# An FNet block with a GeGLU feed-forward on one core: two places for GpSimd's sums, two loads a step sooner, one tile of the second DFT a step later

## The chip, the cores and the metric

The kernel runs on one core of a Trainium2 chip. The metric is the time of one execution on the device, in microseconds (us). The engines of a core have short names in the profile: PE is TensorE (PEld its weight loads), DVE is VectorE, ACT is ScalarE, POOL is GpSimd and SP is SyncE, whose instruction queue issues every DMA of this kernel. Each engine works through its own instructions strictly in the order of the program and waits on semaphores for the others; so does SP, and a DMA that has to wait for a free buffer holds up every DMA behind it.

## The reference

```python
x = A_x                                    # 2048 x 448
n = layernorm(x)
a = n @ dft_hid_re.T ; b = n @ dft_hid_im.T      # DFT along the hidden dimension
h = x + dft_seq_re @ a - dft_seq_im @ b          # DFT along the sequence, real part
g = layernorm(h)
out = h + (gelu(g @ w_gate) * (g @ w_up)) @ w_down   # w_gate, w_up: 448 x 1792
```

All arrays are float32.

## The kernel before, in words

Every product of two float32 matrices is made of three float16 products: each operand is split into a high half (a float16 copy, made by ScalarE in `hi_part`, L107) and a low half (what the copy left out, a float16 made by VectorE in `lo_part`, L110). TensorE takes high by high, high by low and low by high into the same PSUM bank. Splitting the operands in time is what keeps ScalarE and VectorE busy.

The kernel does the DFT along the sequence first, on the normed x (16 tiles `xs` of 128 rows, two halves each), and the DFT along the hidden dimension second. The work before the feed-forward is a loop of 64 steps (`N_STEPS`, L416; the loop is at L848). In each step TensorE multiplies one *unit* of the sequence matrix, 128 x 1024 elements:

- Steps 0 to 15 go over the 16 tiles of x for two of the eight row pairs `p` at once.
- Steps 16 to 31 go over `p` = 2 and 3, eight steps each: four units for `part` 0, four for `part` 1 (`step_of`, L419). A step has 24 matmuls.
- Steps 32 to 63 (`FAST` = 32, L452) do `p` = 4 to 7 with Strassen's seven products on half-size blocks (`fast_mm`, L516; the diff's "seven-product passes"). A step has 42 matmuls. For this the unit needs sums of its blocks (`fast_sums`, VectorE), its raw blocks split (`fast_raw`) and the sums split (`fast_split`); and x needs sums of its own, the T operands of `xs`: for each of the eight pairs `j` of x tiles, `t_sums(j)` (L567) makes them on GpSimd in seven operations, in place in the two arrays `tx[j]`; `t_hi(j)` (ScalarE) and `t_lo(j)` (VectorE) split them.

**Units and slots.** `seq_load(n)` (L424) puts unit n, in two halves for n of 16 and more, into one of the five slots of the tag `wr`; the sums of a seven-product unit take a slot of the same five. The loop (L859) loads unit n+5 in step n, up to unit 33; from unit 34 on, the loads stand behind `fast_split`, two units ahead. The step whose code prepares a seven-product unit is in `fast_at` (L812): step 28 for unit 32, 30 for unit 33, 31 for unit 34, and from step 33 on unit n+2.

**Tiles of the second DFT.** Row pair `p` gives a tile of 256 rows, in two halves g = 0 and 1. When `p` is through, `z_turn(p)` (L662) transposes its result by four DMA transposes into the one tile `z`. `hid_seed(p, g)` (L705, the copy at L708) is a ScalarE copy of the residual x into a PSUM bank; `hid_mm(p, g)` (L720) adds 21 matmuls to it; `hid_out(p, g)` (L710) has ScalarE copy the bank out as h, with its sum (L716), scale the mean (L717) and sum the squares (L718). Both halves use the single bank `tr`, so `hid_seed(p, 1)` stands behind `hid_out(p, 0)`. `ffn_rstd` (L198; a root on ScalarE, a reciprocal on VectorE, the rest on GpSimd), `h_store` and, for the first four tiles, the operands of the feed-forward follow: `ffn_bias` (GpSimd), `ffn_norm_act` (ScalarE), `ffn_sums` (VectorE), `ffn_split` (ScalarE and VectorE) and four DMA transposes `ffn_transpose`. Tiles `p` = 0 to 3 are also called pairs (0,0), (0,1), (1,0) and (1,1) there; "pair 1" is (0,1).

**Weights.** Eight of the fourteen column blocks f of the gate and up weights are prepared during these steps (`DFT_F`, L745): loaded, summed, split in two parts and stored.

**The order** is written out by hand in two tables: `early[n]` is done in step n ahead of its matmuls, `after[n, half]` behind the first or second half of them. What is entered first is done first. For tile p, the lists at L780 to L796 give the step `m` of `hid_mm(p, 0)`, the place `last` of `hid_mm(p, 1)`, and the steps n0, n1, n2 of norm, sums and split. `m1`, one step behind `last`, places `ffn_rstd` and `h_store`. `t_sums(j)` is in `early`, `t_hi(j)` behind the second half of that step, `t_lo(j)` behind the first half of the next.

**The place of `tx`.** Before the change it is one tile under the tag `xh2`, so `t_sums` of one pair waits until `t_lo` of the pair ahead has read it. The x tiles (tag `xt`, three slots) are last read in step 13.

After the 64 steps come the gate and up products (L1321 onward) and the down products with the output; the change does not touch them.

Of the kernel before, what the change touches and what calls it, by code (L numbers as in the profile page):

```python
# [9 lines left out]
F32 = mybir.dt.float32  # L10
# [3 lines left out]
P = 128  # L14
S, D, DF = 2048, 448, 1792
# [17 lines left out]
def kernel(  # L33
# [45 lines left out]
    ring = ctx.enter_context(tc.tile_pool(name="ring", bufs=2))  # L79
# [215 lines left out]
    def ffn_split(q, j):  # L295
        ffn_hi(q, j)
        ffn_lo(q, j)
# [15 lines left out]
    dft = seq.enter_context(tc.tile_pool(name="dft", bufs=1, side="right"))  # L313
# [51 lines left out]
    xt, xs, norm_x = {}, {}, {}  # L365
# [53 lines left out]
    def step_of(n):  # L419

        k, qq = divmod(n - NT, 4)
        return 2 + k // 2, k % 2, qq

    def seq_load(n):  # L424
        wr[n] = dft.tile([P, 8 * P], F32, tag="wr", bufs=5, name=f"wr{n}")
        if n < NT:
            nc.sync.dma_start(wr[n].rearrange("p (b t) -> p b t", b=4), w_seq[8 * (n % 2) + n // 2])
            return
        p, part, qq = step_of(n)
        for i in range(2):  # L430
            dst = wr[n][:, i * 4 * P : (i + 1) * 4 * P].rearrange("p (g t) -> p g t", g=2)
            nc.sync.dma_start(dst, w_seq[8 * p + 2 * qq + i][:, 2 * part : 2 * part + 2, :])
# [19 lines left out]
    FAST = N_STEPS - 32  # L452
# [112 lines left out]
    tx = {}  # L565

    def t_sums(j):  # L567
        t = ring.tile([P, 2, D], F32, tag="xh2", bufs=1, name=f"tx{j}")
        tx[j] = [t[:, k] for k in range(2)]
        for k in range(2):  # L570
            i = 2 * j + 1 - k
            G.tensor_add(tx[j][k], xs[i][:, 0], xs[i][:, 1])  # L572
        (o1, o2), (e1, e2) = [(t[:, 0:HD], t[:, HD:D]) for t in tx[j]]
        G.tensor_sub(o1, o2, o1)
        G.tensor_sub(o2, e2, o2)
        G.tensor_sub(e2, o1, e2)
        G.tensor_add(e1, e1, e2)
        G.tensor_scalar(e1, e1, -1.0, None, op0=ALU.mult)
# [120 lines left out]
    def h_tile(q, j):  # L699
        hp[q, j] = pair_tile(f"hx{q}_{j}", 2 * (q - 2) + j if q > 1 else j)  # L700
        nc.sync.dma_start(hp[q, j], xr[q // 2, 2 * (q % 2) + j])
# [3 lines left out]
    def hid_seed(p, g):  # L705

        y = ys[p, g] = ps_tr.tile([P, 512], F32, tag="tr", name=f"y_{p}_{g}")
        A.activation(y[:, :D], hp[p // 2, p % 2][:, g, :], AF.Copy, scale=sign_of(p, g) * D_SC)  # L708
# [31 lines left out]
    def h_store(q, j):  # L740
        nc.sync.dma_start(h_dram[2 * q + j], hp[q, j])
# [8 lines left out]
    def at(where, n, *what):  # L750
        where.setdefault(n, []).extend(what)
# [26 lines left out]
    for p, (n, half) in enumerate(turns):  # L778
        b, j = divmod(p, 2)
        m = (19, 24, 29, 36, 44, 52, 60)[p]  # L780
        last = ((20, 0), (25, 0), (30, 0), (38, 0), (48, 0), (56, 0), (61, 1))[p]
        m1 = last[0] + 1
        at(early, m - 4, lambda b=b, j=j: h_tile(b, j))
        at(early, m - 2, lambda p=p: hid_seed(p, 0))
        for g in range(2):

            place = last if g else (m, 0)
            at(after, place, lambda p=p, g=g: hid_mm(p, g), lambda p=p, g=g: hid_out(p, g))
            if g == 0:
                at(after, (m, 0), lambda p=p: hid_seed(p, 1))  # L790
        at(after, (n, half), lambda p=p: z_turn(p))
        at(early, m1 + p // 3 if p < 5 else N_STEPS - 7 + p, lambda b=b, j=j: ffn_rstd(b, j))
        at(after, (m1, 0), lambda b=b, j=j: h_store(b, j))
        if b < 2:

            n0, n1, n2 = ((21, 22, 23), (26, 27, 29), (36, 37, 38), (44, 45, 46))[p]  # L796
            at(early, n0, lambda b=b, j=j: ffn_bias(b, j), lambda b=b, j=j: ffn_norm_act(b, j, hp[b, j]))
            at(early, n1, lambda b=b, j=j: ffn_sums(b, j))
            at(early, n2, lambda b=b, j=j: ffn_split(b, j))
            for k in range(4):  # L800
                at(after, (n2 + 1 + k // 2, k % 2), lambda b=b, j=j, k=k: ffn_transpose(b, j, (k,)))
# [1 line left out]
    at(after, (N_STEPS - 6, 0), lambda: gu.update({JIT_F[0]: Weights(JIT_F[0], JIT_F[0] % 3)}))  # L803
    at(early, N_STEPS - 1, gelu_table)
    at(after, (N_STEPS - 2, 0), lambda: down_load(0), lambda: down_load(1))
    for j, n in ((6, 14), (7, 16), (0, 18), (1, 20), (4, 22), (5, 24), (2, 28), (3, 31)):
        at(early, n, lambda j=j: t_sums(j))
        at(after, (n, 1), lambda j=j: t_hi(j))
        at(after, (n + 1, 0), lambda j=j: t_lo(j))
# [38 lines left out]
    for n in range(N_STEPS):  # L848
        if n == 0:
            for key in first:  # L850
                seq_acc(*key, last=key == first[-1])
        elif n >= FAST and n % 4 == 0:
            fast_begin(n)
        elif n >= NT and n % 4 == 0:
            for g in range(2):
                seq_acc(*step_of(n)[:2], g)
        if n + 3 < NT:
            x_load(n + 3)
        if n + 3 < FAST:  # L859
            seq_load(n + 5)  # L860

        if 0 < n < FAST - 3:
            seq_hi(n + 3)
        if 0 < n < NT - 2:
            x_rstd(n + 2)
            x_hi(n + 2)
            x_norm(n + 2)
        if 0 < n < NT - 3:
            x_stats(n + 3)
        if n == 0:  # L870
            seq_lo(2)
        if n + 3 < FAST:
            seq_lo(n + 3)
        if n in fast_at:
            unit = fast_at.index(n) + FAST
            fast_sums(unit)
            while last_lo:
                last_lo.pop()()

            if n < FAST or n % 4 < 3:  # L880
                fast_raw(unit)
                fast_split(unit)
                if unit + 2 < N_STEPS:
                    seq_load(unit + 2)
        if n == 0:
            x_stats(3)
            x_lo(2)
        if 0 < n < NT - 2:
            x_lo(n + 2)
        for what in early.get(n, ()):  # L890
            what()
        if n >= FAST:

            last = n % 4 == 3
            one = [(i, k) for k in range(7) for i in range(2)] if last else [(i, k) for i in range(2) for k in range(7)]
            if n % 4 == 0 and n > FAST:

                one = [(i, k) for i in range(2) for k in range(5)] + [(i, k) for i in range(2) for k in (5, 6)]  # L900
            for m, (i, k) in enumerate(one):
                fast_mm(n, i, k)
                if last and i == 1 and k in (0, 2, 4, 6):
                    fast_out(n, k)
                    if n < N_STEPS - 1:
                        unit = n + 2
                        if k == 2:
                            fast_raw(unit)
                        elif k == 4:
                            fast_split(unit)  # L910
                            if unit + 2 < N_STEPS:
                                seq_load(unit + 2)
                if m in (6, 13):
                    for what in after.get((n, m // 7), ()):
                        what()
            continue

        if n < NT:
            one = [(key, n - n % 2 + key[0], 2 * (2 * key[1] + key[2]) + n % 2, n) for key in first]
            if n == 0:  # L920

                order = [(0, m) for m in (0, 2, 1)] + [(1, m) for m in range(3)]
                one = [(*a, (m,)) for jj, m in order for a in one[4 * jj : 4 * jj + 4]]
            elif n < 6:
                one = [(*a, (m,)) for m in (0, 2, 1) for a in one]
            else:
                one = [(*a, range(3)) for a in one]
        else:
            p, part, qq = step_of(n)
            one = [  # L930
                ((p, part, g), n, 4 * i + 2 * g + c, 4 * qq + 2 * i + c, range(3))
                for i in range(2)
                for g in range(2)
                for c in range(2)
            ]
            if qq == 3:

                one.sort(key=lambda a: a[0])
        for half in range(2):
            for key, unit, block, c, terms in one[half * len(one) // 2 : (half + 1) * len(one) // 2]:  # L940
                seq_mm(key, ws[unit], block, c, terms)
                if c == NT - 1 and 2 in terms and (n < NT or block in (5, 7)):
                    z_out(*key)
            for what in after.get((n, half), ()):
                what()
# [376 lines left out]
    for t in range(NF):  # L1322
        w = gu.get(t + 2) if t + 2 in JIT_F else None
        n = PREP_AT.get(t)
# [88 lines left out]
    for t in range(NF, N_GU):  # L1413
# [37 lines left out]
        if ends:  # L1451
            p = now[-1] // NC
# [21 lines left out]
        for p, t0 in ended.items():  # L1474
            each = 3 if p < 3 else 2
            n = each * (t - t0)
# [106 lines left out]
```

## Time and profile before

| | us |
|---|---|
| median of 3 runs (lowest, highest) | 709.0 (708.27, 710.05) |
| the profiled execution | 708.71 |
| its span, first to last instruction | 706.9 |
| TensorE busy | 695.0 |
| VectorE busy | 571.7 |
| ScalarE busy | 393.7 |
| GpSimd busy | 163.4 |

The mean granted TensorE clock was 0.995 of full speed. All times in the profile are counted from the start of the span. A row of a timeline gives start, duration, engine, line, operation, what it writes and reads, and how many instructions were merged; brackets at its end give the idle time of the engine just before it and what ended that. A row of the waits gives the waiting engine and line, what it waited for, the total, the number of times and the longest.

### The profile page before, as it was taken

Reading aid. Unit: us, or ns where it says so; the run is one execution under the profiler, and the core shown is the slowest. Engines: PE = TensorE matmul, PEld = TensorE weight load, DVE = VectorE, ACT = ScalarE, POOL = GpSimd, SP = SyncE. Lnnn points to the kernel's source line nnn. Section 1 sums busy time; section 2 is a strip of 40 time slices with the busy share of each in tenths; the row PEclk is TensorE's granted clock in tenths of the full one; section 3 lists DMA queues with packets and bytes.
Section 4 is the critical chain, followed back from the end, with each engine's and each line's share of the span. In section 5 each row is a group of like instructions: output and inputs, shape, how many; then the busy total and the mean of one; then the engine's idle time right before and its main releaser. Section 6 shows DMA issues by size and latency. Waiting matters only on the chain.

```text
span 706.9 us, 13957 instructions
## 1 busy us (share of the span) xinstructions
PE 695.0 (98%) x5308; PEld 514.2 (73%) x5308; DVE 571.7 (81%) x1137; ACT 393.7 (56%) x781; POOL 163.4 (23%) x183
## 2 busy tenths in 40 slices
PE   9999999997999999999999999999999999999998
PEld 5555545553788899888744444469999999999997
DVE  7998887969599898997456798877778876899886
ACT  5776555556566475654536666655546454555531
POOL 0004447540300100000213333511020111232224
PEclk9999999998999999999999999999999999999999
DMA  8788759997655829575674878797778985877612
GB/s 273 239 239 287 204 188 275 283 274 235 142 172 153 209 76 208 168 185 168 169 235 156 288 248 262 205 312 236 243 236 300 259 283 177 314 284 259 240 54 79
DMA packets 113731, 155.81 MB, mean 220 GB/s; under 512 B 61696, under 2 KB 78208, under 8 KB 113664
## 3 DMA queue, kind: packets, MB, share of 16 engines
q1 hardware_dynamic: 113664, 154.92, 71.3%
q8 instruction: 41, 0.67, 0.4%
q14 instruction: 26, 0.21, 0.1%
HBM read 106.66 MB, written 34.34 MB: 199 GB/s over the span
## 4 chain that ended last, share of the span: by engine, by line
PE 82%; DVE 4%; DMA 4%; POOL 3%; SPq 2%; ACT 2%; issue 2%; DVEq 0%; ACTq 0%; POOLq 0%
PE acc_f L521 17%; PE acc_d L1245 15%; PE pY L1041 15%; PE acc L641 10%; PE pX L1041 9%; PE pZ L1041 9%; PE y L727 7%; DMA wr<-in_w_seq_dram 2%; DVE gu_w L114 1%; POOL tx L572 1%; DMA gu_raw<-in_w_gu_dram 1%; DVE zs L114 1%; DMA w_dram<-gu_w 1%; SPq L666 1%; DVE t L112 1%
## 5 line engine op out<-in xcount | busy, mean ns | idle before, releaser
L1041 PEld LDWEIGHTS <-gw 128*128 128x128 f16 x1365 | 133.1, 98 | 43.0 <-DMA gw<-w_dram 0.2
L641 PE MATMUL acc<-xs,ws 128*128 128x448 f16 x768 | 146.6, 353 | 0.3 <-DVE xs L149 0.3
L521 PEld LDWEIGHTS <-ws 128*128 128x128 f16 x1344 | 128.8, 98 | 3.2 <-issue 1.6
L641 PEld LDWEIGHTS <-ws 128*128 128x128 f16 x768 | 75.0, 98 | 70.6 <-ACT ws L108 0.4
L1135 POOL TENSOR_TENSOR hs<-hs,c 128x256 f32<-128x256 f32 (+1 forms) x42 | 59.9, 1426 | 247.2 <-ACT c L1133 182.3
L1245 PE MATMUL acc_d<-wd,dn_w 128*128 128x224 f16 x1008 | 110.7, 259 | 0.0
L1245 PEld LDWEIGHTS <-dn_w 128*128 128x128 f16 x1008 | 96.9, 98 | 1.9
L521 PE MATMUL acc_f<-t,ws 128*128 128x224 f16 x768 | 92.1, 259 | 1.4 <-DVE t L112 1.4
L1041 PE MATMUL pY<-hops,gw 128*128 128x256 f16 (+1 forms) x595 | 90.2, 294 | 0.0
L114 DVE SCALAR_TENSOR_TENSOR ws<-wr,ws 128x768 f16<-128x768 f32 (+2 forms) x66 | 71.0, 1077 | 19.0 <-ACT ws L108 18.6
L727 PE MATMUL y<-wh,z 128*128 128x448 f16 x336 | 68.6, 362 | 5.6 <-ACT y L708 5.6
L521 PE MATMUL acc_f<-xs,ws 128*128 128x224 f16 x576 | 73.5, 259 | 0.0
L108 ACT ACTIVATE ws<-wr 128x768 f16<-128x768 f32 (+2 forms) x66 | 60.3, 914 | 11.7 <-DMA wr<-in_w_seq_dram 11.1
L1041 PE MATMUL pX<-hops,gw 128*128 128x256 f16 (+1 forms) x385 | 61.7, 294 | 0.0
L1041 PE MATMUL pZ<-hops,gw 128*128 128x256 f16 (+1 forms) x385 | 61.7, 294 | 0.0
L727 PEld LDWEIGHTS <-z 128*128 128x128 f16 x336 | 33.5, 100 | 37.1 <-issue 9.0
L1086 ACT ACTIVATE pY<-pX 128x256 f32<-128x256 f32 (+1 forms) x42 | 18.4, 439 | 67.0 <-PE pX L1041 66.6
L108 ACT ACTIVATE ws<-sums 128x512 f16<-128x512 f32 x64 | 38.6, 623 | 25.2 <-DVE sums L471 20.8
L1051 DVE SCALAR_TENSOR_TENSOR c<-pZ,u 128x256 f32<-128x256 f32 (+1 forms) x42 | 21.5, 511 | 35.6 <-PE pZ L1041 19.6
L1041 PEld LDWEIGHTS <-gu_w 128*128 128x128 f16 x273 | 26.6, 98 | 31.9
L1097 ACT ACTIVATE u<-pY 128x256 f32<-128x256 f32 (+1 forms) x42 | 19.1, 454 | 53.3 <-PE pY L1041 53.2
L112 DVE TENSOR_TENSOR dn_w<-dn_s,dn_w 128x640 f16<-128x640 f32 x48 | 42.3, 880 | 1.5 <-ACT dn_w L108 1.4
(146 smaller groups left out, 1003.5 us busy)
## 6 DMA issues: line engine op xcount, KB each, us to landing
gw<-w_dram SPq DMA_DIRECT2D x35, 896.0 KB, 6.4
wr<-in_w_seq_dram SPq DMA_DIRECT2D x100, 256.0 KB, 4.1
hid_dram<-hs SPq DMA_DIRECT2D x27, 512.0 KB, 6.0
hid<-hid_dram SPq DMA_DIRECT2D x54, 256.0 KB, 5.4
w_dram<-gu_w SPq DMA_DIRECT2D x14, 896.0 KB, 4.7
gu_raw<-in_w_gu_dram SPq DMA_DIRECT2D x28, 384.0 KB, 5.3
wr<-in_w_seq_dram SPq DMA_DIRECT2D x14, 512.0 KB, 5.6
x<-in_x_dram SPq DMA_DIRECT2D x16, 224.0 KB, 4.0
```

Source lines behind the costliest of these rows:

```text
L108: A.activation(dst, src, AF.Copy, scale=scale)
L112: V.tensor_sub(dst, src, hi)
L114: V.scalar_tensor_tensor(dst, src, scale, hi, op0=ALU.mult, op1=ALU.subtract)
L521: PE.matmul(fast_sum(n, k), fast_a(n, i, lw, a), fast_b(j, lx, b), start=j == 0 and m == 0 and k in (0, 1, 3, 5), stop=j == NT // 2 - 1 an ...
L641: PE.matmul(acc[key][:, :D], w[:, lw, block * P : (block + 1) * P], xs[c][:, lx, :], start=c == 0 and m == 0, stop=c == NT - 1 and m == 2,)
L727: PE.matmul(y[:, :D], z[p][:, lz, k, g * P : (g + 1) * P], wh[:, lw, k, :], start=p == NP - 1 and k == 0 and m == 0, stop=k == 6 and m == ...
L1041: PE.matmul(ps, w[:, wl, wa + ws, :], ops[:, m + ms, :], start=first and n == 0, stop=last and n == len(terms) - 1, skip_group_check=True,)
L1051: V.scalar_tensor_tensor(dst, ps, SC, other, op0=ALU.mult, op1=ALU.add)
L1086: A.activation(self.Y, self.X, AF.Copy)
L1097: A.activation(self.u2, self.Y, AF.Copy, scale=SC)
L1135: G.tensor_mul(c22, c22, self.cols(self.c12))
L1245: PE.matmul(ps, w[:, la, a, :], wd[n][:, lb, b, :], start=n == 0 and m == 0 and opens, stop=n == NC - 1 and m == 2, skip_group_check=True,)
```

## The change

- `t_sums` uses the `xh2` tile for the first, third, fifth and seventh pair of its order (6, 7, 0, 1, 4, 5, 2, 3), and two slots of the `xt` ring for the others.
- The last `t_sums` (pair 3) is entered in step 30 instead of 31, and with it its `t_hi` and `t_lo`.
- `hid_mm(2, 1)` and its `hid_out` stand behind the first half of step 31 instead of 30; with them `ffn_rstd(1, 0)` and `h_store(1, 0)` move from step 31 to 32.
- For pair 1, `ffn_bias` and `ffn_norm_act` move from step 26 to 27, `ffn_sums` from 27 to 28, `ffn_split` from 29 to 32, and the four transposes from behind steps 30 and 31 to behind 33 and 34.
- Step 26 loads units 31 and 32, step 27 loads unit 33, step 28 none by this loop. Before, they were loaded one each in steps 26, 27 and 28 (units 31, 32 and 33).

```diff
     def t_sums(j):
-        t = ring.tile([P, 2, D], F32, tag="xh2", bufs=1, name=f"tx{j}")
-        tx[j] = [t[:, k] for k in range(2)]
+        if len(tx) % 2 == 0:
+            t = ring.tile([P, 2, D], F32, tag="xh2", bufs=1, name=f"tx{j}")
+            tx[j] = [t[:, k] for k in range(2)]
+        else:
+            tx[j] = [dft.tile([P, 1, D], F32, tag="xt", bufs=3, name=f"tx{j}_{k}")[:, 0, :] for k in range(2)]
...
-        last = ((20, 0), (25, 0), (30, 0), (38, 0), (48, 0), (56, 0), (61, 1))[p]
+        last = ((20, 0), (25, 0), (31, 0), (38, 0), (48, 0), (56, 0), (61, 1))[p]
...
-            n0, n1, n2 = ((21, 22, 23), (26, 27, 29), (36, 37, 38), (44, 45, 46))[p]
+            n0, n1, n2 = ((21, 22, 23), (27, 28, 32), (36, 37, 38), (44, 45, 46))[p]
...
-    for j, n in ((6, 14), (7, 16), (0, 18), (1, 20), (4, 22), (5, 24), (2, 28), (3, 31)):
+    for j, n in ((6, 14), (7, 16), (0, 18), (1, 20), (4, 22), (5, 24), (2, 28), (3, 30)):
...
-        if n + 3 < FAST:
-            seq_load(n + 5)
+        for unit in range(n + 5 + (n > FAST - 6), min(n + 6 + (n > FAST - 7), FAST + 2)):
+            seq_load(unit)
```

## The prediction

> **What bounds the kernel now.** I read the page first, then the waits of TensorE, then its timeline around each wait, and last the timelines of ScalarE, VectorE, GpSimd and the DMA queue of SyncE backwards from there.
>
> ```profile
> span 706.9 us, 13957 instructions
> ...
> PE 695.0 (98%) x5308; PEld 514.2 (73%) x5308; DVE 571.7 (81%) x1137; ACT 393.7 (56%) x781; POOL 163.4 (23%) x183
> ```
> ```profile
> PE y L727 <- ACT y L708: 5.6, 2, 4.2
> PE acc_f L521 <- DVE t L112: 1.4, 1, 1.4
> ```
>
> TensorE is busy for 98% of the span, so only its holes can be won. All its waits behind the opening are three: two for a seed of the second DFT (`hid_seed`, L708: the residual, copied into the PSUM bank by ScalarE ahead of `hid_mm`), one for the low half of a T operand (`t_lo`). The change touches what leads up to all three. Their true size is in TensorE's timeline (start, duration, what):
>
> ```profile
> 98.42 4.70 PE L641 MATMUL acc<-xs,ws 128*128 128x448 f16 x24
> 104.53 4.13 PE L727 MATMUL y<-wh,z 128*128 128x448 f16 x21 [1.41 <-ACT y L708]
> ...
> 139.19 18.32 PE L641 MATMUL acc<-xs,ws 128*128 128x448 f16 x96
> 157.35 4.14 PE L727 MATMUL y<-wh,z 128*128 128x448 f16 x21
> 161.33 4.70 PE L641 MATMUL acc<-xs,ws 128*128 128x448 f16 x24
> 170.25 6.53 PE L727 MATMUL y<-wh,z 128*128 128x448 f16 x21 [4.22 <-ACT y L708]
> 176.62 6.97 PE L641 MATMUL acc<-xs,ws 128*128 128x448 f16 x36
> ...
> 189.47 0.74 PE L521 MATMUL acc_f<-xs,ws 128*128 128x224 f16 x6
> 190.04 0.26 PE L521 MATMUL acc_f<-t,ws 128*128 128x224 f16 x1
> 191.72 0.93 PE L521 MATMUL acc_f<-t,ws 128*128 128x224 f16 x8 [1.42 <-DVE t L112]
> ```
> ```profile
> 170.00:176.00 6.00, 5.75 (x18) 2.46 (x18) 5.90 (x12) 2.23 (x4) 0.00 (x0) 0.57 0.77 195
> ...
> 192.00:345.00 153.00, 153.00 (x1435) 137.64 (x1434) 131.30 (x212) 88.61 (x169) 8.08 (x23) 1.00 0.62 169
> ```
>
> A step of 24 matmuls takes (157.35 - 139.19) / 4 = 4.54 us; a `hid_mm` takes 161.33 - 157.35 = 3.98.
> - First seed, tile 0, second half: due at 98.42 + 4.54 = 102.96, started at 104.53. Loss 1.57.
> - Second seed, tile 2, second half: due at 165.87, started at 170.25. Loss 4.38.
> - After it the 21 matmuls took 176.62 - 170.25 = 6.37 instead of 3.98, at a granted clock of 0.57 from 170 to 176. Loss 2.39. (The gaps of about 1.5 us have no such tail.)
> - T operand: six matmuls take 0.57, so the next was due at 190.14 and came at 191.72. Loss 1.58.
>
> (The two rows by window give the busy time of TensorE, its weight loads, VectorE, ScalarE and GpSimd, then the granted clock, the DMA share and GB/s.)
>
> Sum 9.92 us. From 192 to 345 TensorE is busy for 153.00 of 153.00, so what is won before 192 shifts the rest as a whole.
>
> **Part 1, the second `hid_mm` of tile 2 a step later, and pair 1's split from step 29 to 32.** Why was the seed late? ScalarE, with the slots ahead of it:
>
> ```profile
> 159.06 0.84 ACT L108 ACTIVATE ws<-wr 128x768 f16<-128x768 f32 x1 [3.49 <-DMA wr<-in_w_seq_dram]
> ...
> 166.31 0.81 ACT L108 ACTIVATE xs<-xn_h 128x256 f16<-128x256 f32 x2
> ...
> 168.02 0.52 ACT L716 ACTIVATE hx<-y 128x448 f32<-128x448 f32 x1
> ...
> 169.66 0.55 ACT L708 ACTIVATE y<-hx 128x448 f32<-128x448 f32 x1
> ```
>
> Tile 2's first `hid_mm` ended at 161.33, but ScalarE got to its `hid_out` only at 168.02: it had stood 3.49 us for the load of unit 32, and had pair 1's split (166.31 to 168.02, 1.71 us) in front. The seed was there at 170.2. The new place, behind half of step 31, is due 4.54 us later, at 165.87 + 4.54 = 170.41, or 168.84 with the first stall gone. Without the split the seed comes at 170.2 - 1.7 = 168.5 even if nothing else improves. So this stall should go, and the slow clock with it: -4.38 and -2.39.
>
> The step the move issues is 21 matmuls, three ScalarE operations, then the moments, `h_store` and `ffn_rstd`, each a step later. `hid_seed` of tile 3 is at step 34, three steps behind: free. `z_turn(3)` on SP refills the single z tile and must now wait for a `hid_mm` that ends near 172.8, but its last two transposes wait for step 31's own drain, near 176, anyway: free. Behind it on SP stand `h_store` and unit 37's load, needed four steps on.
>
> The split lands in step 32, in front of unit 35 on ScalarE and VectorE. Bounds: on TensorE at least 0; at most its own length if unit 35 is just in time, 1.7 on ScalarE and 2.5 on VectorE:
>
> ```profile
> 167.13 0.42 DVE L112 TENSOR_TENSOR xs<-xn_h,xs 128x256 f16<-128x256 f32 x1
> ...
> 169.64 1.16 DVE L112 TENSOR_TENSOR t<-tx,t 128x448 f16<-128x448 f32 x2
> ...
> 189.56 1.03 DVE L114 SCALAR_TENSOR_TENSOR gu_w<-gu_raw,gu_w 128x512 f16<-128x512 f32 x2 [4.74 <-ACT gu_w L108]
> ...
> 196.31 0.69 DVE L471 TENSOR_TENSOR sums<-wr 128x512 f32<-128x512 f32 x1
> ...
> 198.70 1.22 DVE L114 SCALAR_TENSOR_TENSOR ws<-sums,ws 128x1024 f16<-128x1024 f32 x1
> ```
>
> The split's low halves run from 167.13 to 169.64: 2.5 us. Unit 36 took VectorE from 196.31 to 199.92: 3.6 us for one unit. It was needed at about 201.1: step 32 opened at 176.62 + 36 x 0.189 = 183.4, so 70 of the 84 matmuls of steps 32 and 33 were through by 190.14; the other 14 and two steps of 42, at 0.0955 each, follow on 191.72. That is 1.2 us of slack, and no wait. In the new order step 32 opens at 183.4 - 1.57 - 4.38 - 2.39 = 175.1. Step 31's last drain is out some 1.4 later by my estimate (a copy and a subtraction); from 176.5 I walk VectorE: 1.03 for half a gate weight, 2.5 for the split, 3.6 for unit 35: 183.6. Step 35 is due at 175.1 + 3 x 4.0 = 187.1. Slack 3.5, more than it had. I take 0.
>
> **Part 2, units 32 and 33 loaded a step sooner.** The same loads, moved on SP past the load of weights for f = 0 and the store of pair 1 (which come about 1 us later; the weights are wanted at step 30), and unit 33 past the store of weights for f = 3:
>
> ```profile
> 148.90 1.08 SPq L432 DMA_DIRECT2D wr<-in_w_seq_dram  x2
> 150.08 1.01 SPq L323 DMA_DIRECT2D gu_raw<-in_w_gu_dram  x2
> 151.19 0.38 SPq L741 DMA_DIRECT2D h_dram<-hx  x1
> 151.61 1.44 SPq L432 DMA_DIRECT2D wr<-in_w_seq_dram  x2
> ```
>
> Unit 32 goes out at 150.0 instead of 151.6, ahead of 768 + 448 KB. It landed at 159.06; I estimate 155.5 to 157.5. Bounds: 0 to 3.49 us off ScalarE's wait. The five slots are handed out in the same order, and the slots in question hold units 27 and 28, read two steps before, so nothing new is waited for. On TensorE it is worth 0 by itself, since part 1 already covers the seed; it makes the margin.
>
> **Part 3, two places for GpSimd's sums; the last ones at step 30.** The odd ones go into the ring of x tiles, dead since step 13.
>
> ```profile
> 178.59 0.19 POOL L204 TENSOR_SCALAR r_h<-mv_h 128x2 f32<-128x2 f32 x1 [20.70 <-ACT y L718]
> ...
> 182.71 2.02 POOL L572 TENSOR_TENSOR tx<-xs 128x448 f32<-128x448 f16 x2
> ...
> 187.63 0.77 POOL L578 TENSOR_SCALAR tx<-tx 128x224 f32<-128x224 f32 x1
> ```
>
> The last sums waited in GpSimd's queue behind `ffn_rstd` of tile 2, which waited 20.70 us for `hid_out`; their low halves came at 191.7. Now they are queued ahead of that and have their own place: ready near 164, due at step 33's second half, near 182. -1.58, with 15 us to spare.
>
> ```profile
> POOL tx L572 <- DVE t L112: 19.9, 2, 11.8
> ```
> ```profile
> 99.61 0.58 ACT L108 ACTIVATE t<-tx 128x448 f16<-128x448 f32 x1 [2.06 <-POOL tx L578]
> ...
> 102.29 0.53 ACT L716 ACTIVATE hx<-y 128x448 f32<-128x448 f32 x1
> ...
> 103.93 0.55 ACT L708 ACTIVATE y<-hx 128x448 f32<-128x448 f32 x1
> ```
> ```profile
> 134.63 0.55 ACT L708 ACTIVATE y<-hx 128x448 f32<-128x448 f32 x1
> ```
>
> GpSimd waited 19.9 us for its one place, and ScalarE, in order, for GpSimd. The longest of its waits was 11.8; without them the high half at 99.61 is done some 10 us sooner; tile 0's `hid_out`, at 102.29, can follow TensorE's end at 98.42 closely, and with the 2.2 us from 102.29 to the seed's end it is there at about 101, before 102.96. -1.57. Less sure: tile 1's seed ended at 135.18, just when TensorE wanted it (139.19 - 3.98 = 135.21); it must come 1.57 us earlier as well, or the stall returns there.
>
> What part 3 adds is company: the second sums now run from about 69 to 77, beside VectorE's work ahead of the drain of step 15.
>
> ```profile
> 69.74 1.23 DVE L114 SCALAR_TENSOR_TENSOR ws<-wr,ws 128x1024 f16<-128x1024 f32 x1 [0.32 <-DMA wr<-in_w_seq_dram]
> ...
> 75.36 2.33 DVE L114 SCALAR_TENSOR_TENSOR zs<-acc,zs 128x448 f16<-128x448 f32 x4 [0.59 <-ACT zs L108]
> ```
> ```profile
> L328 DVE TENSOR_TENSOR gu_s<-gu_raw x14: 544/556/1014, 70.9 to 441.2; 128x384 f32<-128x384 f32 x14
> ```
>
> An operation of 0.556 at the median took up to 1.014. Of the 5.0 us that VectorE works between 69.74 and its wait of 0.59, the factor 1.8 makes 0 to 4.1 more; I take 2.5, as not all will meet a sum. The first bank was emptied at 75.36 + 0.58 and is wanted at step 16's opening, 98.42 - 3.98 - 3.5 x 4.54 = 78.6: slack 2.6. I put 0.3 on TensorE, between 0 and 1.5. [...]
>
> **Sum.** 4.38 + 2.39 + 1.58 + 1.57 - 0.3 = 9.6 us. The profiled execution took 708.71 (span 706.9), 0.3 under the median of 709.0; on the median it gives 709.0 - 9.6 = 699.4.
>
> **Rivals.**
> - A, the first stall is given back, at tile 0's seed or at tile 1's: 699.4 + 1.57 = 701.0. For: 135.18 against 135.21. Against: ScalarE's waits for GpSimd go ahead of both. 0.14.
> - B, a new wait at units 35 to 37: VectorE comes late to step 32, the split in front. 2 to 4.4 us, if the clock holds: 701.4 to 703.8. For: 1.2 us of slack before. Against: the walk above. 0.12.
> - C, the change doesn't do what it says: unit 32 lands no sooner behind full queues, TensorE's earlier arrival uses up the step, and the seed is as late as before; only the T operand's 1.58 is won: 707.4. Against: the split alone makes 1.7. 0.05.
> - D, slower: SP becomes the bound. Pair 1's four transposes now stand between the loads of units 37, 38 and 39, and wait for the split. It decides once SP gets to unit 38 after about 193 (step 38 is due near 203: 187.1 + 3 x 4.0 + 3.98; less 3.6 of preparation and, by the 159.06 - 151.61 of unit 32, up to 7 of landing); I expect 184 to 187, as its slot is emptied with unit 35's raw half near 183. Past that point three units in a row would each cost a stall of 4.4 and 2.4 of slow clock: 699.4 + 20 = 720. 0.04.
> - E, the sums shut VectorE out. The seven operations of one tile take 182.71 to 188.40, 5.7 us; if VectorE stood still for them all between 69 and 77, the first bank would come at 75.36 + 5.7 + 0.58 - 0.59 = 81.05, 2.5 after it is wanted: 699.4 + 2.5 - 0.3 = 701.6. For: the 1.014. Against: GpSimd's own operations stretch as well, so the two share the loss. 0.05.
>
> **How the numbers follow.** Forecast 0.60, its own range 698.0 (708.27, the fastest run, less 9.92, rounded down) to 700.4. Nine tenths of that, A, E and two thirds of B lie between 698.0 and 703.0: 0.54 + 0.14 + 0.05 + 0.08 = 0.81. A measurement here tells about 0.3%, 2.1 us, from no change: forecast, A, B and E are faster (0.91), C is the same (0.05), D slower (0.04).
>
> **What would show it.** TensorE's waits should list neither L708 nor `t` behind L521; the second `hid_mm` of tile 2 should take 4.1 near 169; the granted clock should stay at 1.00 from 157 to 192; step 32 should open near 175 instead of 183.2; GpSimd's last sums should be done by 165; the wait of 3.49 on ScalarE should shrink. I am wrong if a new wait for `ws` or `sums` stands between 175 and 205, or if L708 is there again at 102 or 133.

## The result

| | before | changed |
|---|---|---|
| median, us (lowest, highest; 4 runs each) | 709.05 (708.27, 710.05) | 699.6 (698.65, 699.91) |
| ratio to before, 95% interval | | 0.9864 (0.9847 to 0.9881) |
| the profiled execution, us | 708.71 | 699.87 |
| its span, us | 706.9 | 698.1 |

The forecast was 699.4. The head of the page of the changed kernel, and all its waits of TensorE (waiting engine and line, what it waited for, total, times, longest):

```profile
span 698.1 us, 13955 instructions
...
PE 693.5 (99%) x5308; PEld 514.3 (74%) x5308; DVE 571.2 (82%) x1137; ACT 394.1 (56%) x781; POOL 166.6 (24%) x183
```
```profile
PE pw L102 <- POOL sign_t L93: 1.4, 1, 1.4
PE acc_d L1248 <- ACT v L974: 0.2, 1, 0.2
```

The three waits of before are gone; what is left stands in the opening and near the end, and both stood there before too (three lines were added, so L708 is now L711, L727 is L730 and so on). TensorE's timeline at the places of the old holes:

```profile
99.03 4.70 PE L644 MATMUL acc<-xs,ws 128*128 128x448 f16 x24
103.57 4.13 PE L730 MATMUL y<-wh,z 128*128 128x448 f16 x21
...
160.32 9.24 PE L644 MATMUL acc<-xs,ws 128*128 128x448 f16 x48
169.59 4.13 PE L730 MATMUL y<-wh,z 128*128 128x448 f16 x21
173.56 2.43 PE L644 MATMUL acc<-xs,ws 128*128 128x448 f16 x12
175.83 0.74 PE L521 MATMUL acc_f<-xs,ws 128*128 128x224 f16 x6
```

Tile 0's second half starts at 99.03 + 4.54 = 103.57, the moment it is due. Tile 2's second half is due at 160.32 + 9.08 = 169.40 and starts at 169.59: 0.2 is left of 4.38. It takes 3.97 at a granted clock of 1.00 from 157 to 192, so the slow clock is gone too. Step 32 opens at 175.83 instead of 183.4.

The time adds up to within 0.1. Of 9.92 us of holes 9.72 are gone. Against that, TensorE reached its first `hid_mm` 0.61 later in this execution (95.06 against 94.45; 0.23 of it ahead of the first product), and two small waits are new, in the weight loads of the seven-product passes:

```profile
253.13 1.17 PEld L521 LDWEIGHTS <-ws 128*128 128x128 f16 x13 [0.31 <-DVE ws L114]
265.28 9.22 PEld L521 LDWEIGHTS <-ws 128*128 128x128 f16 x97 [0.21 <-DVE ws L114]
```

The nine matmuls behind each of these two waits took 1.26 and 1.16 where such nine take 1.03, so TensorE lost 0.4. 9.72 - 0.61 - 0.4 = 8.7, against 708.71 - 699.87 = 8.84 measured. But the ScalarE rows ahead of the second seed are not those that the prediction drew:

```profile
157.57 0.84 ACT L108 ACTIVATE ws<-wr 128x768 f16<-128x768 f32 x1 [1.73 <-DMA wr<-in_w_seq_dram]
...
165.36 1.04 ACT L108 ACTIVATE t<-tx 128x448 f16<-128x448 f32 x2 [3.97 <-DMA w_dram<-gu_w]
...
167.35 0.52 ACT L719 ACTIVATE hx<-y 128x448 f32<-128x448 f32 x1
...
168.99 0.55 ACT L711 ACTIVATE y<-hx 128x448 f32<-128x448 f32 x1
```

Unit 32 did come sooner (157.57 for 159.06). Then a wait that the kernel before did not have held ScalarE for 3.97 us: `t_hi(2)` writes into the slot w1, and that slot was still being read by the store of the weights f = 3. The seed was done at 169.54, 0.14 after the matmuls were due. SP's rows (start, duration of the issue) say why; the first is the load of units 31 and 32, the fourth that of unit 33:

```profile
150.46 2.03 SPq L432 DMA_DIRECT2D wr<-in_w_seq_dram  x4
152.58 0.85 SPq L323 DMA_DIRECT2D gu_raw<-in_w_gu_dram  x2
153.53 0.38 SPq L744 DMA_DIRECT2D h_dram<-hx  x1
153.95 1.52 SPq L432 DMA_DIRECT2D wr<-in_w_seq_dram  x2
155.57 0.74 SPq L362 DMA_DIRECT2D w_dram<-gu_w  x1
```

The same two places in the kernel before, the store on SP and `t_hi(2)` on ScalarE:

```profile
153.15 0.78 SPq L362 DMA_DIRECT2D w_dram<-gu_w  x1
```
```profile
164.34 1.03 ACT L108 ACTIVATE t<-tx 128x448 f16<-128x448 f32 x2
```

The store now stands behind unit 33's load and is issued at 155.57 instead of 153.15, in part because SP came to the first of these loads 1.56 later (150.46 for 148.90). So the whole landed where it was forecast, while one part seemed to work against it. The experiments are about that.

### The profile page after: what moved, and what is told of

It reads as the page before. It is cut to its first block, busy times and chain, and to the rows that moved or that the text cites. A ratio compares the mean times of both kernels' runs of the same rounds, so it can differ in the third digit from the quotient of the medians.

```text
span 698.1 us, 13955 instructions
## 1 busy us (share of the span) xinstructions
PE 693.5 (99%) x5308; PEld 514.3 (74%) x5308; DVE 571.2 (82%) x1137; ACT 394.1 (56%) x781; POOL 166.6 (24%) x183
## 4 chain that ended last, share of the span: by engine, by line
PE 96%; ACT 1%; DVE 1%; issue 1%; POOL 0%; ACTq 0%; POOLq 0%
PE acc L644 21%; PE acc_f L521 16%; PE acc_d L1248 15%; PE pY L1044 15%; PE pZ L1044 10%; PE pX L1044 10%; PE y L730 9%; PE pw L102 1%; ACT ws L108 1%; DVE ws L114 0%; ACT xn_h L243 0%; DVE sums L471 0%; ACT dn_w L108 0%; ACT v L974 0%; ACT y L721 0%
## 5 line engine op out<-in xcount | busy, mean ns | idle before, releaser
L114 DVE SCALAR_TENSOR_TENSOR ws<-wr,ws 128x768 f16<-128x768 f32 (+2 forms) x66 | 73.8, 1119 | 10.4 <-ACT ws L108 10.1
L730 PE MATMUL y<-wh,z 128*128 128x448 f16 x336 | 66.2, 352 | 0.0
L730 PEld LDWEIGHTS <-z 128*128 128x128 f16 x336 | 32.9, 98 | 29.5 <-issue 0.3
```

The lines of the kernel that those rows point to most:

```text
L114: V.scalar_tensor_tensor(dst, src, scale, hi, op0=ALU.mult, op1=ALU.subtract)
L730: PE.matmul(y[:, :D], z[p][:, lz, k, g * P : (g + 1) * P], wh[:, lw, k, :], start=p == NP - 1 and k == 0 and m == 0, stop=k == 6 and m == ...
```

## The experiments

| label | what is left of the change | median us | ratio, 95% interval |
|---|---|---|---|
| e1 | tile's step, split's move | 706.52 | 0.9962 to 0.9981 |
| e2 | two places, last sums at 30 | 705.35 | 0.9940 to 0.9965 |
| e8 | earlier loads | 708.53 | 0.9992 to 1.0010 |
| e10 | tile's step, split's move, last sums at 30 | 702.69 | 0.9908 to 0.9935 |
| e4 | all but the tile's step | 704.93 | 0.9939 to 0.9965 |
| e6 | all but the second place | 701.88 | 0.9892 to 0.9922 |
| e5 | all but the split's move | 700.10 | 0.9869 to 0.9896 |
| e3 | all but the earlier loads | 699.19 | 0.9854 to 0.9880 |
| e7 | all, but unit 33 loaded in step 28 | 698.91 | 0.9851 to 0.9877 |
| e9 | two places, last sums at 30, tile's step | 699.59 | 0.9861 to 0.9888 |
| e11 | the changed kernel again | 699.03 | 0.9853 to 0.9880 |

Each ratio is to runs of the kernel before on the same chip (medians 708.45 for e1 to e4, 708.58 for e5 to e8, 708.54 for e9 to e11). The changed kernel itself came to 699.6 and 699.03 on two occasions, so 0.6 us between rows of this table tells nothing.

**e1, the tile and the split alone.**

```diff
-        last = ((20, 0), (25, 0), (30, 0), (38, 0), ...
+        last = ((20, 0), (25, 0), (31, 0), (38, 0), ...
-            n0, n1, n2 = ((21, 22, 23), (26, 27, 29), ...
+            n0, n1, n2 = ((21, 22, 23), (27, 28, 32), ...
```

> The kernel before with only tile 2's second half a step later and pair 1's operands moved (step 29 to 32); one place for GpSimd's sums, last sums at step 31, loads as before. Theory H (three separate holes, the second cured by the step and the split): the second seed is there near 168.5 and due near 170.4, so its 4.38 and the slow tail of 2.39 go: 709.05 - 6.77 = 702.3 with the wait for the T operand still there, or 700.7 if moving ffn_rstd to step 32 is by itself enough to let the last sums pass on GpSimd; the first seed's 1.57 stays in both. Rival G (the two places free ScalarE, and that is what brings the seed in time): the second hole shrinks by no more than the split's 1.7, 706 or more. Rival L (the earlier load of unit 32 does it): a hole of 1 to 4 us stays, 703 to 707.

Measured 706.52: none of the three theories. The time is one that G allowed, but the second hole is gone, as H has it and G has not (the seed's row at 166.56, and 3.97 for the `hid_mm`). What grew is the T operand's hole. TensorE of this run, then VectorE:

```profile
183.66 0.26 PE L521 MATMUL acc_f<-t,ws 128*128 128x224 f16 x1
187.64 1.65 PE L521 MATMUL acc_f<-t,ws 128*128 128x224 f16 x8 [3.72 <-DVE t L112]
```
```profile
181.42 0.62 DVE L114 SCALAR_TENSOR_TENSOR zs<-acc,zs 128x448 f16<-128x448 f32 x1 [0.54 <-ACT zs L108]
...
183.81 0.42 DVE L112 TENSOR_TENSOR xs<-xn_h,xs 128x256 f16<-128x256 f32 x1
...
186.44 1.14 DVE L112 TENSOR_TENSOR t<-tx,t 128x448 f16<-128x448 f32 x2
```

TensorE came to that operand 6.4 us sooner (183.76 for 190.14), but its low halves, entered behind half of step 32, stood on VectorE behind the drain of step 31 (181.42) and behind the very split that had been moved into step 32 (from 183.81). The hole is 187.64 - 183.76 = 3.9 instead of 1.58, and the 20 matmuls behind it ran slowly, 1.6 more (granted clock 0.63 from 188 to 192). Most of what part 1 won went there.

**e10, the same with the last sums at step 30.**

```diff
-... (2, 28), (3, 31)):
+... (2, 28), (3, 30)):
```

> The run with only the tile and the split moved, and now the last sums at step 30 too (still one place, loads as before). Theory Q (there the low half of the last T operand stood on VectorE behind the moved split and the drain of step 31, 3.9 us late with a slow tail): one step sooner it stands ahead of both, the T operand's hole of 5.5 us goes, the first seed's 1.57 stays, 708.5 - 6.8 - 1.6 = 700.1 to 701.9. Rival (with one place the last sums themselves are too late): a hole above 2 us stays, 703 or more.

Theory Q holds for the hole: the waits of this run no longer list the T operand, only the first seed.

```profile
PE y L727 <- ACT y L708: 1.4, 1, 1.4
```

The median, 702.69, lies 0.8 above the range expected; the profiled execution took 701.26, within it. Its runs spread up to 704.11 although the granted clock reads 1.00 in all five, where kernels with a slow tail read 0.994 to 0.998. So a slow tail is not likely the reason; no profile shows what is, and it is open.

**e2, the places and the last sums alone; e4, all but the tile's step.**

```diff
# e2, on the kernel before: t_sums as in the changed kernel, and
-... (2, 28), (3, 31)):
+... (2, 28), (3, 30)):
# e4, on the changed kernel
-        last = ((20, 0), (25, 0), (31, 0), (38, 0), ...
+        last = ((20, 0), (25, 0), (30, 0), (38, 0), ...
```

> The kernel before with only the two places for GpSimd's sums and the last sums at step 30. H: the first seed's 1.57 and the T operand's 1.58 go, the second hole stays whole: 709.05 - 3.15 = 705.9. G: the second hole goes or shrinks to below 2 us as well: 702 or less. L: as H.

> The changed kernel with tile 2's second half back behind half of step 30. H: the seed comes where it came in the changed kernel, near 169.5, and is due at 160.3 + 4.5 = 164.9: a hole of 4.6 and a slow tail of 2.4, 706.6. G and L (ScalarE is early enough without the step): a hole under 2 us and no tail, 700 to 701.5.

e2 came to 705.35 for 705.9: H. e4 came to 704.93 for 706.6: the hole is back, a little smaller than I had it, as the seed ended at 168.1 in this run. TensorE, e2 first, then e4:

```profile
160.43 4.70 PE L644 MATMUL acc<-xs,ws 128*128 128x448 f16 x24
168.83 6.92 PE L730 MATMUL y<-wh,z 128*128 128x448 f16 x21 [3.70 <-ACT y L711]
175.58 6.97 PE L644 MATMUL acc<-xs,ws 128*128 128x448 f16 x36
```
```profile
160.08 4.70 PE L644 MATMUL acc<-xs,ws 128*128 128x448 f16 x24
168.12 6.92 PE L730 MATMUL y<-wh,z 128*128 128x448 f16 x21 [3.33 <-ACT y L711]
174.88 6.97 PE L644 MATMUL acc<-xs,ws 128*128 128x448 f16 x36
```

e4: due at 160.08 + 4.54 = 164.62, started 3.5 late, then 174.88 - 168.12 = 6.76 for what takes 3.97. The gap is followed by a slow `hid_mm` in both, so the other edits, together as they are in e4, don't remove these 6 us, and the step does. Part of this hole is the loads' own doing, though: in e4 ScalarE stood 3.36 us for the store of f = 3. The step at 30 without the earlier loads was not run; by an estimate from e3, where the seed is done at 167.0 and step 30's place would be due at 160.18 + 4.54 = 164.7, a hole of about 2.3 would be left, and no run shows whether a gap of that length has a slow tail.

**e3, all but the earlier loads; e7, unit 33 alone put back; e8, the loads alone.**

```diff
# e3, on the changed kernel (e8: the reverse, on the kernel before)
-        for unit in range(n + 5 + (n > FAST - 6), min(n + 6 + (n > FAST - 7), FAST + 2)):
-            seq_load(unit)
+        if n + 3 < FAST:
+            seq_load(n + 5)
# e7: units 31 and 32 in step 26, none in 27, 33 in 28
+        for unit in range(n + 5 + (n == FAST - 5), min(n + 6 + (n == FAST - 6), FAST + 2)):
```

> The changed kernel with the loads of units 31, 32 and 33 back in steps 26, 27 and 28. H: the loads gave margin only, 699.6 within 0.5; the wait of 3.97 us that ScalarE had for the store of the weights f = 3 (behind unit 33's load in the changed kernel) goes, so the second seed may come earlier than its 169.5. L: the seed is late by 1.5 to 4 us: 701.1 to 704. G: as H.

> The changed kernel with unit 32 still loaded in step 26 but unit 33 back in step 28, behind the store of the weights f = 3. Theory S (it is unit 33's load ahead of that store that makes ScalarE wait 3.97 us, as t_hi(2) writes into the slot that the store reads): the wait is gone or under 1 us, the second seed comes at 166 to 167, and no hole: 699.3. Rival (the store is late because unit 32's load and the full queues hold it up): the wait stays above 2.5 us.

> The kernel before with only the loads of units 32 and 33 a step sooner. Theory S: unit 32 lands a little sooner, but ScalarE waits for the store instead; the second hole keeps its size within 1.5 us, 708.5 (707.5 to 710). Rival L (the earlier load brings the seed in): the hole shrinks by 2 us or more, 706.5 or less.

ScalarE at `t_hi(2)` and at the second seed, e3 first, then e7:

```profile
162.82 1.04 ACT L108 ACTIVATE t<-tx 128x448 f16<-128x448 f32 x2 [0.32 <-DMA w_dram<-gu_w]
...
166.45 0.55 ACT L711 ACTIVATE y<-hx 128x448 f32<-128x448 f32 x1
```
```profile
162.35 1.05 ACT L108 ACTIVATE t<-tx 128x448 f16<-128x448 f32 x2 [1.16 <-DMA w_dram<-gu_w]
...
165.98 0.55 ACT L711 ACTIVATE y<-hx 128x448 f32<-128x448 f32 x1
```

Without the earlier loads the seed is done at 167.0, 2.5 us *sooner* than with them. With only unit 33 back behind the store (issued at 153.09), it is done at 166.5. The wait in e7 is 1.16, a little above the 1 us that theory S allowed, and far below the rival's 2.5. SP came to these loads at 149.55 in e7 and at 150.46 in the changed kernel, but that is not what decides: in e4, with all the loads early, SP came at 149.38, the store was issued at 154.39, and the wait was 3.36. So it is unit 33's place ahead of the store that cost the wait. No run tells the times of the three kernels apart.

In e8, the kernel before with the loads alone, unit 32 was there early, and ScalarE stood at the next thing:

```profile
156.15 0.84 ACT L108 ACTIVATE ws<-wr 128x768 f16<-128x768 f32 x1 [0.33 <-DMA wr<-in_w_seq_dram]
162.11 0.63 ACT L108 ACTIVATE ws<-sums 128x512 f16<-128x512 f32 x1 [5.11 <-DVE sums L471]
...
169.71 0.55 ACT L708 ACTIVATE y<-hx 128x448 f32<-128x448 f32 x1
```

The wait of 3.49 for the load turned into 5.11 for VectorE, which had other work ahead of the sums, and the seed came at 170.26, as before. The time, 708.53, is no other than before. Not the store, as theory S had it for this run, but VectorE held ScalarE here.

**e5 and e9, the split back in step 29, with and without the earlier loads.**

```diff
-            n0, n1, n2 = ((21, 22, 23), (27, 28, 32), ...
+            n0, n1, n2 = ((21, 22, 23), (26, 27, 29), ...
```

> The changed kernel with pair 1's bias, norm, sums and split back in steps 26, 27 and 29 (transposes behind 30 and 31). Theory M (the second seed hangs on what ScalarE has in front of it, and in the changed kernel it comes at 169.5 with 0.1 us to spare): the split's 1.7 us in front bring the seed to about 171.2, a hole of 1.5 to 2 us without a slow tail, 701.2. Rival R (the step alone gives enough room): no hole, 699.6.

> The changed kernel without the earlier loads and with pair 1's operands back in steps 26 to 29: of the change only the two places, the last sums at step 30 and the tile's step are left. If the loads are what makes the split's move necessary (by the store they delay): the seed comes at 167.0 + 1.7 = 168.7, due 169.3, no hole, 699.2. Rival (the split's move is needed in any case): a hole of 1 us or more, 700.2 or more.

TensorE of e5, and ScalarE's seed in e9:

```profile
170.24 4.13 PE L730 MATMUL y<-wh,z 128*128 128x448 f16 x21 [0.95 <-ACT y L711]
```
```profile
168.44 0.55 ACT L711 ACTIVATE y<-hx 128x448 f32<-128x448 f32 x1
```

With the loads early, the split in front makes a hole of 0.95 without a slow tail (the `hid_mm` behind it took 174.21 - 170.24 = 3.97): M, at half the size. (The seed of the changed kernel had no 0.1 us to spare, it was 0.14 late.) The median, 700.10, lies nearer to R's 699.6 than to M's 701.2; it is the row that decides. Without them the seed is done at 168.99, ahead of its matmuls at 169.15, and no hole is there. So the split's move was needed only because the earlier loads had used the margin up; e9, with neither, takes 699.59.

**e6, one place.**

```diff
-        if len(tx) % 2 == 0:
...
+        t = ring.tile([P, 2, D], F32, tag="xh2", bufs=1, name=f"tx{j}")
+        tx[j] = [t[:, k] for k in range(2)]
```

> The changed kernel with one place for GpSimd's sums (the last sums still at step 30). If the first hole hangs on the one place: TensorE waits for a seed near 103 as before, 1.57 us, and nothing else, 701.2. If the place matters at the end too (the last sums wait for the low half of the pair ahead, near 168, and end near 174): still before their use near 182, so the T operand costs nothing. Rival (the place does nothing, the first hole goes for another reason): 699.6.

701.88 for 701.2. The waits of TensorE in this run:

```profile
PE y L727 <- ACT y L708: 1.4, 1, 1.4
PE pw L102 <- POOL sign_t L93: 1.4, 1, 1.4
PE acc_f L521 <- DVE ws L114: 0.7, 2, 0.4
```

The first seed's wait is back, as expected; 0.7 more go, at 254 and 255, to a unit that VectorE finished late. Beside the last sums (168.37 to 176.60 here) VectorE's work had stretched, an addition of 0.42 to 1.14; at its row for unit 36 it was 2.25 us behind the changed kernel (192.63 for 190.38), where TensorE was 1.22 behind at the `hid_mm` that follows. That this lag is what TensorE met 60 us later is argued, not shown.

**e11, the changed kernel again.**

> The changed kernel again, as it is, beside the others on the same chip: 699.6 within 0.5; the wait for the store on ScalarE between 2.5 and 4.5 us and the second seed 0 to 1 us ahead of its matmuls.

699.03. ScalarE waited 3.29 for the store, and the seed was done at 168.86 for matmuls at 169.40.

## Why the prediction was right, step by step

- **The sum of three holes** held: 699.4 forecast, 699.6 and 699.03 measured. e6 brings back the first hole and e4 the second; the third stands in e1 and is gone in e10, which differs by the step of the last sums alone. The holes are not independent, though. e1 wins 1.9 us and e2 3.1, together 5.0, while e3, which has the edits of both and no others, wins 9.3. The rest comes only with both, since the third hole grows to 5.5 (3.9 and 1.6 of slow matmuls) once the second is gone and the last sums stay at step 31. The prediction added the three because the whole change was the question; taken as three gains for three edits it would have been wrong.
- **First seed**: right in size and cause. GpSimd's wait of 19.9 for its place is 2.7, and ScalarE followed TensorE closely; the rows show tile 0's `hid_out` and seed, then tile 1's seed.

```profile
POOL tx L575 <- DVE t L112: 2.7, 1, 2.7
```
```profile
99.29 0.55 ACT L719 ACTIVATE hx<-y 128x448 f32<-128x448 f32 x1 [3.49 <-PE y L730]
...
100.95 0.55 ACT L711 ACTIVATE y<-hx 128x448 f32<-128x448 f32 x1
...
133.28 0.55 ACT L711 ACTIVATE y<-hx 128x448 f32<-128x448 f32 x1
```

Tile 0's seed is done at 101.50 for matmuls due at 103.57. **Rival A** did not come at tile 1 either, by 0.4: done at 133.83 for 134.22, where it was 135.18 for 135.21.

- **Second seed**: right that it goes, wrong about the margin. "Without the split the seed comes at 170.2 - 1.7 = 168.5 even if nothing else improves" left out that something could get worse: it came at 169.54. That only 0.2 of a hole was left was luck; nothing in the prediction made room for the wait that ate the margin. The step of the tile is what removes the hole (e4); the split's move is not needed (e9).
- **The earlier loads**: the step "on TensorE it is worth 0 by itself ...; it makes the margin" failed in its second half. I listed the store of f = 3 as one of the DMAs passed on SP and gave it no price: "nothing new is waited for" looked at the slots that the loads write. Who *overwrites* what the store reads was the question: `t_hi(2)`, in the slot w1, in step 28. Price 3.97 us of ScalarE (3.29 in e11), hidden but for 0.2. The load itself did not go out at 150.0 as I had it: SP came late, so unit 32 was issued at 151.57 (151.61 before), and was there at 157.5, the late end of what I gave.
- **T operand**: right that the hole goes, wrong about the room. GpSimd's last sums ran from 153.51 and ended at 160.5, but VectorE got to the low halves only at 178.56 (in the VectorE rows further down) and was done at 179.71 for a use at 175.83 + 6.71 = 182.54: 2.8 us to spare, not 15. The second place is not needed here: e6 and e10 have one place and no wait for `t`.

```profile
153.51 2.02 POOL L575 TENSOR_TENSOR tx<-xs 128x448 f32<-128x448 f16 x2
...
159.71 0.82 POOL L581 TENSOR_SCALAR tx<-tx 128x224 f32<-128x224 f32 x1
```

- **Units 35 and 36 (rival B)**: no wait, but by less than I wrote. VectorE of the changed kernel:

```profile
178.56 1.15 DVE L112 TENSOR_TENSOR t<-tx,t 128x448 f16<-128x448 f32 x2
179.62 0.62 DVE L114 SCALAR_TENSOR_TENSOR zs<-acc,zs 128x448 f16<-128x448 f32 x1
...
185.66 1.22 DVE L114 SCALAR_TENSOR_TENSOR ws<-sums,ws 128x1024 f16<-128x1024 f32 x1
...
190.38 1.22 DVE L114 SCALAR_TENSOR_TENSOR ws<-sums,ws 128x1024 f16<-128x1024 f32 x1
```

Unit 35 is ready at 186.9 for a step due at 175.83 + 12.0 = 187.9: slack 1.0, not 3.5. Unit 36 is ready at 191.6 for 191.93. My walk began with the drain of step 31 at 176.5; it ended at 180.2, as ScalarE had unit 34 and tile 2's `hid_out` in front of it.

- **Company on GpSimd (rival E)**: VectorE came to the drain of step 15 at 78.51 instead of 75.36, 3.15 later (0.41 of it already there at 70.15) where I took 2.5 between 0 and 4.1. TensorE shows no wait there, so no row bears out the 0.3 of the sum; but the first bank was emptied at 79.07 for an opening near 99.03 - 3.97 - 3.5 x 4.54 = 79.17, so 0.1 was left of a slack of 2.6.

```profile
71.95 1.39 DVE L328 TENSOR_TENSOR gu_s<-gu_raw 128x384 f32<-128x384 f32 x1
...
78.51 2.21 DVE L114 SCALAR_TENSOR_TENSOR zs<-acc,zs 128x448 f16<-128x448 f32 x4
```

Both sides stretch: the operation of 0.556 took 1.39, and GpSimd's seven took 69.92 to 78.10, 8.2 us where they take 5.7 alone. VectorE came 3.15 later, not the 5.7 that rival E gave. The 0.61 by which TensorE was later at 95 can't be put down to this: counted from the first product to the first `hid_mm`, the time was 88.58 to 89.14 in the five kernels with one place (before, e1, e6, e8, e10) and 88.70 to 89.14 in the eight profiles with two.

- **C and D** did not come. SP got to unit 38's load at 188.5, later than the 184 to 187 I gave and 4.5 us ahead of the 193 at which D would have begun.

## What to carry to other kernels

A late operand is cured in the queue that makes it late, and the cure is worth only the time until the next late operand: read the next need of the same engine before adding gains up. When a DMA is moved past others on a queue, ask of each store that it passes who wants to overwrite the store's source, as well as who reads its target. A margin is worth measuring even where the time does not show it: here two of the five edits, the earlier loads and the split's move, only paid for each other.

## What the runs showed of the hardware

- The clock behind a gap: behind 0.95 (e5) the `hid_mm` took 3.97, and behind 1.58 (before) and 1.6 (e8) the eight matmuls of `t` took 0.76 and 0.77, so these gaps left the next matmuls at full speed. Gaps of 3.5 (e4), 3.9 (e1, e2) and 4.38 (before) were followed by 2.8, 1.6, 2.8 and 2.39 us of loss at a lower granted clock: 0.57 from 170 to 176 before, 0.63 from 188 to 192 in e1, and, as the mean from 95 to 200, 0.97 in e2 and e4 where the changed kernel has 1.00. The loss does not follow the gap's length: behind 4.39 in e8 it was 2.82. So a hole brought from 3.5 or more to 1.6 or less was worth more than its length here.
- A load moved up on the queue: unit 32 was issued at 152.14 in e3 and at 150.66 in e7, 1.5 us sooner, and ScalarE's copy of it began at 159.31 and 156.93, 2.4 us sooner. In the changed kernel SP was later; unit 32 was issued when it had been before (151.57 and 151.61) and was still there 1.5 us sooner, with the load of f = 0 and the store of pair 1 no longer ahead of it.
- A store and its source: the store of f = 3 was issued at 153.09 in e7 and at 155.57 in the changed kernel; ScalarE wrote into the slot that it reads 9.3 and 9.8 us later, after waits of 1.16 and 3.97 for that store.
